# Where two value blocks of a head group stand: rows of five, or eight groups of eight rows

## The chip, the cores and the metric

The kernel runs on one core of a Trainium2 chip, in one launch. The metric is device time in microseconds. Three runs of the kernel before gave 2576.46, 2576.75 and 2577.24 us. The core has TensorE (PE), VectorE (DVE), ScalarE (ACT), GpSimd (POOL) and SyncE (SP), whose instruction queue issues nearly all transfers, and 16 DMA engines that carry them.

## The reference

Two layers, each an attention block over a cache and a gated feed-forward block, for two sequences with one new token each. Everything is float32.

```
x: (2, 1, 512)   k_cache, v_cache: (2, 8, 32768, 128)   wq: (512, 4096)   wo: (4096, 512)

x = x + A(layernorm(x));  x = x + B(layernorm(x));  and both once more, with the same weights and caches

A: q = (x @ wq) as 32 heads of 128;  each of 8 cache heads serves 4 query heads
   p = softmax(q . k * 128**-0.5);  o = p . v;  o @ wo
B: gate = x @ W_gate;  h = gate * (gate > 0) * (x @ W_up);  h @ W_down
```

There are 8 x 2 = 16 head groups (a cache head of one sequence). Each has 16.8 MB of keys and 16.8 MB of values, and both layers read them all: about 1.1 GB go from memory to the chip.

## The kernel before

`attention_reglu_decode` goes through the head groups in the order `seq`, 0 to 15 in layer 0 and 15 to 0 in layer 1, so that the last group of layer 0 is partly kept for layer 1. A head group's keys and its values come in two halves of 128 partitions x 64 KB. One half is one transfer (`pages`, line 94, with `whole`), and one transfer gives each of the 16 DMA engines eight rows. A half is worked on as four pages of 16 KB a row. Where a page is loaded by itself, it is a transfer of its own.

Order of the program: `keys(i)` (line 407) multiplies the queries into both key halves of group i; inside it stand the tail of the softmax of group i - 1 (`soft_tail`, line 248: transposes of the weights, row sums) and the output of group i - 2 (`head_out`, `project`). Then `values(i - 1, ...)` (line 434) multiplies the transposed weights `pT` of the group before into its values, with the softmax of group i behind the first page. Loads are issued by SP in program order, each when its place in the arena is free.

The arena is one tile of 220 units of 1 KB a row. `take` (line 62) gives out units: a half takes 64 of them, so 192 units are three halves in rotation; the 28 units at the end are for small tiles and for the output projection's weights. For loads, the free place that was freed longest ago is taken.

A value *block* is 512 columns (2 KB) of a value row: 128 partitions x 4 keys of 128 numbers. A half has 32 blocks, a group 64. `v_tile` (line 302) does one multiplication for each block: 16 columns of `pT` as weights, 512 columns of values, into the quarter 32c to 32c + 15 of the accumulator `acc`, where c is the block's number modulo 4.

In one group of each layer (`SIDE_HEAD` = 12, the thirteenth in order) three blocks of page 5 are not read as part of the value rows. `values` cuts the page in two pieces around them, and the second half of the group comes in five transfers: 16 KB, 8 KB, 2 KB, 16 KB and 16 KB a row. The 384 rows of these blocks come from an array of their own, `side`, laid out by the host: `load_side` (line 295) issues eight transfers of five rows of 20 KB, each to every fourth partition of a stretch of twenty, two of them ahead of each value piece from page 4 on. `side_keys` (line 265) prepares the softmax weights for those rows (GpSimd clears a part, three transposes and a masking multiplication on VectorE), and `v_side` (line 283) does ten multiplications into `acc` ahead of the last page.

Of the kernel before, what the change touches and what calls it, by code (L numbers as in the profile page):

```python
# [41 lines left out]

SIDE_HEAD, SIDE_PAGE, SIDE_AT, SIDE = 12, 5, 4, 3
SIDE_ROWS, SIDE_CHUNKS = 20, 5

C_SAME, C_SELH, C_PAIR, C_COL, C_SELQ, C_SIDE, C_END = 0, 128, 144, 176, 178, 210, 211


@with_exitstack
def attention_reglu_decode(ctx: ExitStack, tc: tile.TileContext, x, k, v, side, wq, wo, wgu, wd, consts, out):  # L50
# [28 lines left out]
    def done(loaded):  # L79
        clock[0] += 1  # L80
        for u in loaded[1]:
            freed[u] = clock[0]
# [29 lines left out]
    selq = cst[:, C_SELQ : C_SELQ + 32]  # L112
    side_rows = cst[:, C_SIDE : C_SIDE + 1]
    col = cst[:, C_COL : C_COL + NB]
# [150 lines left out]
    def side_keys(p):  # L265
        W = SIDE_CHUNKS * 32
        t = take(2 * W)
        at = SIDE_PAGE // 2 % 2 * D + (SIDE_PAGE % 2 * 8 + SIDE_AT) * 32

        def windows(rows):  # L270
            return bass.AP(rows.tensor, rows.offset + at, [rows.ap[0], [SIDE_ROWS, SIDE_CHUNKS], [1, 32]])

        def chunks(rows):
            return rows.rearrange("p (k r) -> p k r", r=32)

        nc.gpsimd.memset(t[0][64:, W:], 0.0)
        nc.vector.transpose(chunks(t[0][:, :W]), windows(p))
        for c in (0, 32):
            nc.vector.transpose(chunks(t[0][c : c + 32, W:]), windows(p[64 + c : 96 + c]))
        nc.vector.tensor_scalar_mul(t[0], t[0], side_rows[:, 0:1])  # L280
        return t

    def v_side(n, vt):
        t = side_of.pop(n)
        J = SIDE_PAGE // 4
        for k in range(2 * SIDE_CHUNKS):
            nc.tensor.matmul(
                acc[32 * (k % 4) : 32 * (k % 4) + 16, :],
                t[0][:, 32 * k + 16 * J : 32 * k + 16 * J + 16],
                vt[:, k * D : (k + 1) * D],  # L290
                start=False, stop=False,
            )
        done(t)

    def load_side(n, t):
        for c in (0, 32):
            for r in range(4):
                yield nc.sync.dma_start(t[0][c + r : c + SIDE_ROWS : 4], side[n, c // 32, r])

# [103 lines left out]
    for L in range(NLAYER):  # L403
        last = L == NLAYER - 1
        seq = list(range(NG)) if L % 2 == 0 else list(range(NG - 1, -1, -1))

        def keys(i):
            n = seq[i]
            if i < NG - 1:
                place_queries(i + 1, seq[i + 1])  # L410
            if last and i == 0:
                loads = list(kept_k)
                kept_k.clear()
            else:
                loads = pages(k, n, not (last and i == 1))
            for j, t in enumerate(loads):
                k_tile(L, i, n, j, t[0])
                if not last and i == NG - 1:
                    kept_k.append(t)
                else:  # L420
                    done(t)
                if last and i == 0:
                    yield
                if j == 1 and i >= 1:
                    soft_tail(L, seq[i - 1], i == SIDE_HEAD + 1)
# [118 lines left out]
```

## Time and profile before

| | |
|---|---|
| three runs | 2576.46 to 2577.24 us, median 2576.75 |
| span of the profiled execution | 2575.9 us |
| PE, PE weight loads | 1306.1 us (51%), 338.5 us (13%) busy |
| DVE, ACT, POOL | 149.3 us (6%), 41.1 us (2%), 3.4 us busy |
| read from memory | 1105.70 MB |

The span runs from the first to the last instruction of one profiled execution; the runs were timed apart from it, and their median is 0.85 us above it. In the profile a queue row gives packets, megabytes and the time that its packets took as a share of 16 engines' span. A DMA *packet* is one row of a transfer on one engine, or the 4-byte mark with which an engine tells that it is through with its rows. The views of a window count the packets that start in it. In the rows of instructions, `L309 PE MATMUL out<-in shapes xcount | busy, mean ns | idle before` has the engine's idle time just ahead of that group, with what ended it. `SPq` is SP's queue of issues.

### The profile page before, as it was taken

How to read it: one execution, taken by the hardware profiler on the slowest of the kernel's cores; microseconds unless marked ns; L12 is line 12 of the kernel's file. 1: busy time of each engine (PE TensorE's matmuls, PEld its weight loads, DVE VectorE, ACT ScalarE, POOL GpSimd, SP SyncE). 2: the span in 40 equal slices, each digit the busy share in tenths (PEclk: the TensorE clock that was granted, in tenths of full speed). 3: DMA queues.
4: the chain of work that ended last, by engine and by line, in shares of the span. 5: the costliest groups of instructions: out<-in, count | busy, mean ns of one | idle time of the engine just before them, and what ended most of it. 6: DMA issues, size and time to landing. Idle time of an engine off the chain costs nothing.

```text
span 2575.9 us, 19565 instructions
## 1 busy us (share of the span) xinstructions
PE 1306.1 (51%) x9256; PEld 338.5 (13%) x9256; DVE 149.3 (6%) x363; ACT 41.1 (2%) x67; POOL 3.4 (0%) x13
## 2 busy tenths in 40 slices
PE   2544454455445544545675554455445544554456
PEld 0111111111011111111121111111111101111111
DVE  0000000000000000000010000000000000000001
ACT  0000000000000000000000000000000000000000
POOL 0000000000000000000000000000000000000000
PEclk9777777777767777777778677767677777777778
DMA  9999999999999999999999999999999999999999
GB/s 425 432 430 436 430 432 436 431 432 430 434 435 429 437 431 433 420 429 426 424 416 437 430 432 436 432 434 430 434 432 431 436 431 430 436 429 422 436 424 391
DMA packets 31919, 1107.02 MB, mean 430 GB/s; under 512 B 3600, under 2 KB 3984, under 8 KB 7440
## 3 DMA queue, kind: packets, MB, share of 16 engines
q1 hardware_dynamic: 31552, 1105.61, 99.7%
q8 instruction: 72, 1.18, 0.2%
q10 hardware_dynamic: 288, 0.17, 0.0%
q14 instruction: 7, 0.06, 0.0%
HBM read 1105.70 MB, written 0.07 MB: 429 GB/s over the span
## 4 chain that ended last, share of the span: by engine, by line
DMA 68%; PE 23%; another core or an unknown queue 9%; issue 0%; DVE 0%; SPq 0%; ACTq 0%; DVEq 0%
DMA arena<-k 51%; PE sc L225 16%; DMA arena<-v 13%; PE acc L309 5%; DMA cst<-consts 2%; DMA arena<-wd 1%; DMA arena<-wq 1%; PE qp L195 1%; PE po L331 1%; DMA arena<-wgu 1%; PE op L344 0%; PE sm L257 0%; PE mp L239 0%; PE dn L384 0%
## 5 line engine op out<-in xcount | busy, mean ns | idle before, releaser
L225 PE MATMUL sc<-arena,qz 128*32 128x512 f32 x4096 | 589.7, 728 | 602.4 <-DMA arena<-k 602.4
L309 PE MATMUL acc<-arena 128*16 128x512 f32 (+1 forms) x4128 | 585.6, 720 | 587.7 <-DMA arena<-v 587.7
L225 PEld LDWEIGHTS sc<-arena,qz 128*32 128x32 f32 x4096 | 144.0, 131 | 1003.1 <-issue 689.9
L309 PEld LDWEIGHTS acc<-arena 128*16 128x16 f32 x4128 | 119.4, 109 | 1003.4 <-issue 509.9
L235 DVE TENSOR_REDUCE stat<-sc 128x1 f32<-128x1024 f32 x32 | 39.2, 1225 | 648.8 <-PE sc L225 648.8
L245 ACT ACTIVATE arena<-sc,stat 128x1024 f32<-128x1024 f32 x32 | 35.7, 1114 | 2370.3 <-DVE stat L242 2319.5
L325 DVE TENSOR_SCALAR arena<-acc,stat 128x512 f32<-128x512 f32 (+1 forms) x38 | 24.8, 665 | 779.8 <-PE acc L309 779.8
L252 DVE STREAM_TRANSPOSE arena<-arena 128x512 f32<-128x512 f32 x64 | 41.5, 687 | 2.5 <-ACT arena L245 2.5
L331 PE MATMUL po<-cst,arena 128*128 128x4 f32 x256 | 34.8, 259 | 1.9 <-DVE arena L325 1.9
L331 PEld LDWEIGHTS po<-cst,arena 128*128 128x128 f32 x256 | 32.0, 195 | 26.6 <-issue 23.5
L259 DVE RECIPROCAL stat<-sm 128x1 f32<-128x1 f32 x32 | 5.3, 166 | 435.4 <-PE sm L257 435.4
L242 DVE TENSOR_REDUCE stat<-mp 128x1 f32<-128x32 f32 x32 | 6.1, 192 | 360.5 <-PE mp L239 360.5
L362 PE MATMUL gu<-arena 128*32 128x448 f32 x128 | 20.7, 747 | 10.6 <-DMA arena<-wgu 9.4
L195 PE MATMUL qp<-arena 128*32 128x512 f32 x128 | 23.2, 838 | 4.8 <-DMA arena<-wq 2.9
L149 PE MATMUL meana<-stat,ones 128*128 128x2 f32 x4 | 0.9, 298 | 44.2 <-DVE stat L148 44.2
L239 PEld LDWEIGHTS mp<-arena,cst 128*128 128x128 f32 x64 | 13.4, 261 | 52.7 <-issue 51.0
L239 PE MATMUL mp<-arena,cst 128*128 128x32 f32 x64 | 17.3, 359 | 3.4 <-DVE arena L238 1.7
L344 PE MATMUL op<-arena,oT 128*2 128x512 f32 x112 | 14.6, 592 | 3.6 <-DVE oT L334 3.6
L257 PEld LDWEIGHTS sm<-stat,cst 128*128 128x128 f32 x64 | 9.7, 191 | 28.7 <-issue 28.7
L257 PE MATMUL sm<-stat,cst 128*128 128x1 f32 x64 | 12.4, 264 | 0.0
L334 DVE COPY oT<-po 128x4 f32<-128x4 f32 x32 | 5.2, 162 | 76.4 <-PE po L331 76.4
L384 PE MATMUL dn<-arena 128*32 128x512 f32 x32 | 6.8, 937 | 4.7 <-DVE arena L373 3.6
(62 smaller groups left out, 83.7 us busy)
## 6 DMA issues: line engine op xcount, KB each, us to landing
arena<-v SPq DMA_DIRECT2D x31, 2048.0 KB
arena<-wo SPq DMA_DIRECT2D x16, 1024.0 KB
arena<-k SPq DMA_DIRECT2D x8, 2048.0 KB
arena<-wq SPq DMA_DIRECT2D x8, 1024.0 KB
arena<-wgu SPq DMA_DIRECT2D x8, 896.0 KB
arena<-wgu SPq DMA_DIRECT2D x4, 1792.0 KB
arena<-v SPq DMA_DIRECT2D x8, 512.0 KB
arena<-wd SPq DMA_DIRECT2D x4, 1024.0 KB
```

Of the source, the lines that this page charges most:

```text
L195: nc.tensor.matmul(qp[32 * c : 32 * c + 32, B, :], xT[:, kt, :], t[0][:, c * D : (c + 1) * D], start=kt == 0, stop=kt == KT - 1)
L225: nc.tensor.matmul(sc_of[n][32 * c : 32 * c + 32, B, :], qz[:, i % 2, 28 - 4 * j : 60 - 4 * j], kt[:, ch * D : (ch + 1) * D], start=j == 0 ...
L235: nc.vector.tensor_reduce(m1[:, :1], sc_of[n], AX.XY, ALU.max)
L239: nc.tensor.matmul(mp[:, :32], same, mt[0], start=True, stop=True)
L245: nc.scalar.activation(p[0], sc_of[n].rearrange("p a b -> p (a b)"), AF.Exp, bias=nm[:, 0:1], scale=1.0, accum_out=rs[:, :1])
L252: nc.vector.transpose(pT[0][:, B * D : (B + 1) * D], p[0][:, B * D : (B + 1) * D])
L257: nc.tensor.matmul(sm[:, 0:1], same, rs[:, :1], start=True, stop=True)
L309: nc.tensor.matmul(acc[32 * c : 32 * c + 16, e * w : (e + 1) * w], pT[:, B, m, 16 * J : 16 * J + 16], vt[:, at * D + e * w : at * D + (e + ...
L325: nc.vector.tensor_scalar_mul(acs[:, t:e], acc[:, t:e], linv[:, 0:1])
L331: nc.tensor.matmul(po[:, :REP], acs[0][:, t * P : (t + 1) * P], selh[:, 4 * t : 4 * t + 4], start=t == 0, stop=t == 3)
L344: nc.tensor.matmul(op[32 * u : 32 * u + NB, :], oT[:, u, :], w, start=i == 3, stop=i == NG - 1)
L362: nc.tensor.matmul(gu[32 * j : 32 * j + 32, s, :FS], xT[:, kt, :], t[0][:, j * FS : (j + 1) * FS], start=kt == 0, stop=kt == KT - 1)
```

## The change

The one set of three blocks in one group of a layer is replaced by two blocks in each of three groups of a layer: the groups at places 3, 8 and 13 of the order in layer 0, and 4, 9 and 14 in layer 1. The blocks are now the last two of the group's last page. So the second value half stays one transfer, with rows of 60 KB instead of 64 KB, and `v_tile` does six blocks of the last page.

The rows of the two blocks stand on partitions 0 to 63 alone: each of these gets its own two blocks and those of the row 64 further on, 8 KB in all. They come as one transfer of 64 rows, issued behind the second value half; its source is an array laid out by the host as eight groups of eight rows, a little padding between the groups. `side_keys` is two transposes, which put the weights of rows 64 to 127 on partitions 0 to 63; the weights of the rows' own blocks are read from `pT`. `v_side` does four multiplications with 64 rows each, behind the group's last page. GpSimd's clearing, the masking multiplication and its constant column go.

```diff
-SIDE_HEAD, SIDE_PAGE, SIDE_AT, SIDE = 12, 5, 4, 3
-SIDE_ROWS, SIDE_CHUNKS = 20, 5
+SIDE_HEADS, SIDE = ((3, 8, 13), (4, 9, 14)), 2
+HALF_ROW = HALF * PAGE
+SIDE_ROW = HALF_ROW - SIDE * D
+SIDE_PITCH = 8 * 2 * SIDE * D + 64
...
-    def pages(src, n, whole):
+    def pages(src, n, whole, short=False):
         for h in range(NT // HALF):
             if whole:
-                t, us = load(src[n, h])
+                t, us = take(HALF_ROW, False, False)
+                w = SIDE_ROW if short and h else HALF_ROW
+                nc.sync.dma_start(t[:, :w], src[n, h, :, :w])
...
     def side_keys(p):
-        W = SIDE_CHUNKS * 32
-        t = take(2 * W)
-        at = SIDE_PAGE // 2 % 2 * D + (SIDE_PAGE % 2 * 8 + SIDE_AT) * 32
...
-        nc.gpsimd.memset(t[0][64:, W:], 0.0)
-        nc.vector.transpose(chunks(t[0][:, :W]), windows(p))
+        t = take(SIDE * 32)
+        at = 2 * D - SIDE * 32
         for c in (0, 32):
-            nc.vector.transpose(chunks(t[0][c : c + 32, W:]), windows(p[64 + c : 96 + c]))
-        nc.vector.tensor_scalar_mul(t[0], t[0], side_rows[:, 0:1])
+            nc.vector.transpose(t[0][c : c + 32], p[64 + c : 96 + c, at:])
         return t
 
     def v_side(n, vt):
         t = side_of.pop(n)
-        J = SIDE_PAGE // 4
-        for k in range(2 * SIDE_CHUNKS):
+        own = pT_of[n][0][:64, 2 * D - SIDE * 32 :]
+        for k in range(2 * SIDE):
+            keys, m = (own, k) if k < SIDE else (t[0][:64], k - SIDE)
+            c = (8 - SIDE + k) % 4
             nc.tensor.matmul(
-                acc[32 * (k % 4) : 32 * (k % 4) + 16, :],
-                t[0][:, 32 * k + 16 * J : 32 * k + 16 * J + 16],
-                vt[:, k * D : (k + 1) * D],
-                start=False, stop=False,
+                acc[32 * c : 32 * c + 16, :],
+                keys[:, 32 * m + 16 : 32 * m + 32],
+                vt[:64, k * D : (k + 1) * D],
+                start=False, stop=True,
             )
         done(t)
 
-    def load_side(n, t):
-        for c in (0, 32):
-            for r in range(4):
-                yield nc.sync.dma_start(t[0][c + r : c + SIDE_ROWS : 4], side[n, c // 32, r])
+    def load_side(L, i):
+        t = take(2 * SIDE * D, False, False)
+        e = 3 * L + SIDE_HEADS[L].index(i)
+        rows = bass.AP(side.tensor, side.offset + 8 * e * SIDE_PITCH, [[SIDE_PITCH, 8], [2 * SIDE * D, 8], [1, 2 * SIDE * D]])
+        nc.sync.dma_start(t[0][:64], rows)
+        return t
...
-                whole = pages(v, n, last or i < NG - 2)
-                if i == SIDE_HEAD:
-                    pieces[SIDE_PAGE : SIDE_PAGE + 1] = [(SIDE_PAGE, 0, SIDE_AT, None), (SIDE_PAGE, SIDE_AT + SIDE, 8, None)]
-                    whole = islice(whole, HALF)
-            sides = iter(())
+                whole = pages(v, n, last or i < NG - 2, i in SIDE_HEADS[L])
+                if i in SIDE_HEADS[L]:
+                    pieces[-1] = (NT - 1, 0, 8 - SIDE, None)
             for at, (j, lo, hi, t) in enumerate(pieces):
-                if i == SIDE_HEAD and j == HALF:
-                    aside = take(2 * SIDE_CHUNKS * D, False, False)
-                    sides = load_side(L, aside)
-                next(sides, None)
-                next(sides, None)
-                if i == SIDE_HEAD and j == NT - 1:
-                    v_side(n, aside[0])
-                    done(aside)
...
                 if soft is not None and at == 0:
                     soft_max(L, soft)
+                if i in SIDE_HEADS[L] and j == HALF:
+                    aside = load_side(L, i)
+            if i in SIDE_HEADS[L]:
+                v_side(n, aside[0])
+                done(aside)
             evacuate(L, n, i == NG - 1)
```

More of the change, by code (lines that the diff above doesn't have):

```diff
@@ L1 @@
 from contextlib import ExitStack
-from itertools import islice
 import concourse.bass as bass
@@ L112, in attention_reglu_decode @@
     selq = cst[:, C_SELQ : C_SELQ + 32]
-    side_rows = cst[:, C_SIDE : C_SIDE + 1]
     col = cst[:, C_COL : C_COL + NB]
@@ L265, in side_keys @@
     def side_keys(p):
-        W = SIDE_CHUNKS * 32
-        t = take(2 * W)
-        at = SIDE_PAGE // 2 % 2 * D + (SIDE_PAGE % 2 * 8 + SIDE_AT) * 32
[L270 to L277, printed above, removed]
+        t = take(SIDE * 32)
+        at = 2 * D - SIDE * 32
         for c in (0, 32):
-            nc.vector.transpose(chunks(t[0][c : c + 32, W:]), windows(p[64 + c : 96 + c]))
-        nc.vector.tensor_scalar_mul(t[0], t[0], side_rows[:, 0:1])
+            nc.vector.transpose(t[0][c : c + 32], p[64 + c : 96 + c, at:])
         return t
@@ L500 @@
     cst[:, C_PAIR : C_PAIR + 32] = np.equal.outer(rows // 4, np.arange(32))
-    cst[:, C_SIDE] = (rows < 64) & (rows % 32 < SIDE_ROWS)
     cst[:, C_COL : C_COL + NB] = np.equal.outer(rows % 32, np.arange(NB))
@@ L509, in by_block, with side_blocks @@
         return con(w.reshape(4, KT, 32, -1).transpose(1, 0, 2, 3)).reshape(KT, P, -1)
-    def side_blocks(vc):
-        sets = []
-        J, B, m = SIDE_PAGE // 4, SIDE_PAGE // 2 % 2, SIDE_PAGE % 2 * 8 + SIDE_AT
+    def side_blocks(v):
+        sets = np.zeros((NLAYER * 3, 8, SIDE_PITCH), np.float32)
         for L in range(NLAYER):
-            n = SIDE_HEAD if L % 2 == 0 else NG - 1 - SIDE_HEAD
-            keys = vc[n % NB, n // NB].reshape(2, 4, 2, 4, 512, DH)[J, :, B, :, 32 * m : 32 * (m + SIDE)]
-            rowsets = np.zeros((4, 4, SIDE_CHUNKS * SIDE_ROWS, DH), np.float32)
-            rowsets[:, :, : 32 * SIDE] = keys.transpose(1, 0, 2, 3)
-            t = rowsets.reshape(2, 2, 4, SIDE_CHUNKS, SIDE_ROWS // 4, 4, DH)
-            sets.append(t.transpose(1, 5, 4, 0, 3, 2, 6).reshape(2, 4, SIDE_ROWS // 4, -1))
-        return con(np.stack(sets))
+            for e, i in enumerate(SIDE_HEADS[L]):
+                n = i if L % 2 == 0 else NG - 1 - i
+                t = v[n, 1, :, SIDE_ROW:].reshape(2, 64, -1).transpose(1, 0, 2)
+                sets[3 * L + e, :, : 8 * 2 * SIDE * D] = t.reshape(8, -1)
+        return sets
     wq = con(a["A_wq"].reshape(D, 2, HKV * REP // 2, 4, 32).transpose(0, 1, 3, 2, 4)).reshape(D, -1)
@@ L528 @@
         "v": con(a["A_v_cache"].reshape(NB, HKV, 2, 4, 2, 4, 16, 32, DH).transpose(1, 0, 2, 5, 7, 4, 6, 3, 8)).reshape(NG, 2, P, SK // 2),
-        "side": side_blocks(a["A_v_cache"]),
+        "side": None,
         "wq": con(by_block(wq).reshape(KT, P, 2, -1).transpose(1, 2, 0, 3)).reshape(P, -1),
@@ L535 @@
     }
+    arrays["side"] = side_blocks(arrays["v"])
     nc = bacc.Bacc("TRN2", target_bir_lowering=False, num_devices=1, dynamic_dma_scratch_size=SCRATCH)
```

4 lines of the change are left out of this document (2 added, 2 removed).

## The prediction

> **What bounds the kernel now.** I read the page first: the DMA digits, the queues, the chain.
>
> ```profile
> span 2575.9 us, 19565 instructions
> ...
> DMA  9999999999999999999999999999999999999999
> ...
> DMA packets 31919, 1107.02 MB, mean 430 GB/s; under 512 B 3600, under 2 KB 3984, under 8 KB 7440
> ...
> q1 hardware_dynamic: 31552, 1105.61, 99.7%
> q8 instruction: 72, 1.18, 0.2%
> ...
> DMA 68%; PE 23%; another core or an unknown queue 9%; issue 0%; DVE 0%; SPq 0%; ACTq 0%; DVEq 0%
> ```
>
> The kernel's own transfers (q1) keep 16 DMA engines busy for 99.7% of the span, so what counts is how many microseconds of work the most loaded engine gets. The rate of one engine follows from the q1 row: 0.997 x 16 x 2575.9 us / 1105.61 MB = 37.17 us per MB, so 32 KB take 1.22 us, 48 KB 1.83, 64 KB 2.44, 160 KB 6.09. The q8 row is the second user: 72 transfers of 16.4 KB that carry instructions.
>
> Whether all engines are loaded alike can't be read from a mean. But the packets under 512 B are nearly all completion marks, one for each engine and transfer, so counting them in narrow windows shows how far apart the engines run. The first three windows of the DMA view are 138:139, 139:139.5 and 139.5:141 (a 128-row transfer of value rows ends there), then the q8 row of 0:138.5; the next three are 1002:1003.4, 1003.4:1006.4 and 1006.4:1009.2 (another such transfer), then the q8 row of 0:1002; then 1062.5:1066.8.
>
> ```profile
> DMA packets 27, 0.92 MB, mean 918 GB/s; under 512 B 13, under 2 KB 13, under 8 KB 13
> DMA packets 0, 0.00 MB, mean 0 GB/s; under 512 B 0, under 2 KB 0, under 8 KB 0
> DMA packets 16, 0.85 MB, mean 568 GB/s; under 512 B 3, under 2 KB 3, under 8 KB 3
> q8 instruction: 3, 0.05, 0.1%
> ...
> DMA packets 21, 0.85 MB, mean 609 GB/s; under 512 B 8, under 2 KB 8, under 8 KB 8
> DMA packets 17, 1.11 MB, mean 371 GB/s; under 512 B 0, under 2 KB 0, under 8 KB 0
> DMA packets 26, 1.18 MB, mean 421 GB/s; under 512 B 8, under 2 KB 8, under 8 KB 8
> q8 instruction: 26, 0.43, 0.2%
> ...
> DMA packets 80, 1.74 MB, mean 406 GB/s; under 512 B 18, under 2 KB 18, under 8 KB 18
> ```
>
> After three instruction transfers three engines are late. After 26 of them eight engines finish within 1002.0 to 1003.4, none for three microseconds, and the other eight at 1006.4 to 1009.2. So the instruction transfers fall on **eight engines in turn**, 26/8 = 3.25 each by then, and every core instruction that waits for a whole transfer waits for those eight. The last window says where the old five-row transfers stand: 18 marks, eight of a 128-row transfer and ten of two five-row ones, while the loaded eight are not through with the transfer ahead. So all five engines of the five-row transfers are among the eight light ones.
>
> **The price of one instruction transfer** to its engine. The window 60.5:62 has one alone:
>
> ```profile
> q8 instruction: 1, 0.02, 4.2%
> ```
>
> Its own packet takes 0.042 x 16 x 1.5 = 1.0 us. From the lateness: the middles of the two groups of marks are 1007.8 and 1002.7, 5.1 us for 3.25 transfers, 1.57 each; some of that can be an offset from the start. I take 1.5 us, near the second row, since lateness is what is paid; bounds 1.0 and 1.6. Over the run a loaded engine gets 72/8 = 9 of them: 13.5 us (9.0 to 14.4).
>
> [...]
>
> **The change, part by part.** All sums are work on one engine over both layers.
>
> ```profile
> arena<-side SPq DMA_DIRECT2D x16, 100.0 KB
> ```
>
> *Before.* In one head group of each layer three blocks of 2 KB rows leave the value rows: 8 rows x 6 KB = 48 KB less on each of 16 engines, 2 x 1.83 = 3.65 us. In their place come eight transfers of five 20 KB rows. The page's 3600 marks agree with five engines for each: 220 transfers x 16 + 16 x 5 = 3600. Those five get 160 KB a layer, 2 x 6.09 = 12.18 us. Against a kernel without any of this: loaded eight 13.5 - 3.65 = **+9.85 us**; five light ones 12.18 - 3.65 = +8.53; the other three -3.65. The loaded eight are the bound.
>
> *Removed and added transfers.* Both five-row sets and their gaps in the value rows go. In six head groups two blocks leave the last half: 8 rows x 4 KB = 32 KB less on every engine, 6 x 1.22 = 7.31 us. One transfer of 64 rows of 8 KB takes their place. Its source is written as eight groups of eight rows. By the marks, a transfer of five rows used five engines; I take eight engines with eight rows each, 64 KB, 6 x 2.44 = 14.62 us, and that they are the light ones. The other end: sixteen engines with four rows, 32 KB each.
>
> [...] The trace shows the five; no run here shows an eight yet.
>
> *The sum.* Loaded eight: 13.5 - 7.31 = +6.19. Light eight: 14.62 - 7.31 = **+7.31**. The light eight become the bound, by 1.1 us, and the end moves by 7.31 - 9.85 = **-2.54 us**. With 1.6 us an instruction transfer the old bound is 10.75 and the gain 3.44. With 1.0 the old bound is the five light engines' 8.53, and the gain 1.2; but then they, not the loaded eight, would have been last.
>
> *Number of transfers.* Eight pieces of value rows fewer (two halves that were cut in five are whole again), sixteen five-row ones fewer, six more. q1 and q8 together fill 99.9%, so the gaps are at most 0.1% x 2575.9 = 2.6 us for some 220 transfers: 0.01 us each, nothing to 0.2 us in all. I take nothing.
>
> *SP's queue.* The sixteen issues on line 298 leave, and with them a stall; then the halves:
>
> ```profile
> 1000.12 0.33 SPq L76 DMA_DIRECT2D arena<-k  x1
> ...
> 1050.72 9.93 PE L225 MATMUL sc<-arena,qz 128*32 128x512 f32 x64 [10.15 <-DMA arena<-k]
> 1050.75 19.98 SPq L298 DMA_DIRECT2D arena<-side  x2
> ...
> SPq L298 <- DMA arena<-k: 44.7, 4, 12.6
> SPq L298 <- DMA arena<-v: 43.1, 4, 18.6
> ```
>
> In the old stage SP waited 44.7 + 43.1 us on line 298 with the next value pieces queued behind it. The light engines can run dry there; the loaded ones were 3 to 7 us behind and had work, so I count nothing back. The new transfer is one issue directly behind the second value half; the next key half is queued behind it. Its 8 units come from the small end of the arena, by the allocator's oldest-freed rule either never used or last used by an output-projection tile of an earlier head pair, long read; so no wait of its own. If it did wait, the cover is the lead: the half issued at 1000.12 is first used at 1050.72, and a half of 8 x 64 KB takes 19.5 us, so 31 us of queued work cover a late issue.
>
> *TensorE.* The new multiplications run behind the last value tile of a head.
>
> ```profile
> L309 PE MATMUL acc<-arena 128*16 128x512 f32 (+1 forms) x4128 | 585.6, 720 | 587.7 <-DMA arena<-v 587.7
> L287 PE MATMUL acc<-arena 128*16 128x512 f32 x40 | 5.5, 592 | 0.0
> ...
> 328.89 47.59 DMA arena<-v
> ...
> 376.53 9.10 PE acc L309 x64
> ```
>
> Twenty calls (40 rows in the trace, two for each call) become 24, and six value blocks fewer go through line 309 (12 instead of 6 left out): two calls fewer in all. PE idles 10.15 us ahead of the half above, 587.7 us before line 309 in all; cost nothing. The side rows can land up to 2.44 us behind the last half; PE then has the 9.10 us of that half to do first. So PE does not wait for them. Uncovered, it would be at most 2.44 us in six places, 14.6 us.
>
> *VectorE and GpSimd.*
>
> ```profile
> L279 DVE STREAM_TRANSPOSE arena<-arena 32x160 f32<-32x160 f32 x4 | 1.3, 334 | 0.1
> L280 DVE TENSOR_SCALAR arena<-arena,cst 128x320 f32<-128x320 f32 x2 | 0.8, 386 | 0.2
> L277 DVE STREAM_TRANSPOSE arena<-arena 128x160 f32<-128x160 f32 x2 | 0.6, 302 | 0.0
> L276 POOL MEMSET arena<- 64x160 f32 x2 | 0.5, 227 | 163.3 <-PE acc L309 163.3
> ```
>
> 2.7 us of DVE and 0.5 of GpSimd in two places become two smaller transposes in six places, at most 12 x 0.334 = 4.0 us, 0.67 a head. They sit in front of the reciprocal and behind the two transposes that PE needs, in the 10 us before a half lands. Cost nothing; without that cover 0.67 x 6 - 2.7 = 1.3 us.
>
> *The end.* The last issue stands 2.6 us ahead of the span's end and follows the last weights; it moves with them.
>
> ```profile
> 2573.29 0.35 SPq L485 DMA_DIRECT2D out<-x  x1
> ```
>
> The sum is made against the span: 2575.9 - 2.5 = 2573.4. The runs' median is 2576.75, 0.85 above the span, and I keep that distance: **2574.2 us**. Single light engines also carry a few other instruction packets and marks, worth up to a microsecond: 2573.0 to 2575.6.
>
> **Rivals.**
> 1. *The two groups take turns*: where a layer ends everything waits for everything, and each layer has its own worst engine. A layer has up to five instruction transfers on one engine: 7.5 - 1.83 = 5.67 before; 7.5 - 3.65 = 3.85 after, and the light eight 3.65. Twice the difference: 3.65 us, 2573.1. For it: the many small weight transfers between the layers. Against it: 72/8 is nine, not ten.
> 2. *The eight engines are not the light ones* (slower). The five-row rows prove five light engines only. If the eight of the new transfer take three loaded ones, each of these has 13.5 + 7.31 = 20.8, 11.0 above the old bound: 2587.7. It decides from the first loaded engine in the set. For it: nothing names the other three. Against it: five of five were light, and sixteen engines in a light and a loaded eight are most simply the first and the last eight.
> 3. *It does not do what it says*: the 64 rows go to all 16 engines, four each. Then 32 KB come back where 32 KB left, the loaded eight stand at 13.5, 3.65 above before: 2580.4. For it: 64 divides by 16. Against it: the outer count of the source is eight.
> 4. *Instruction transfers cost the data nothing.* Then the five light engines' 8.53 was the bound, and becomes 7.31: -1.2 us, 2575.5. Against it: the eight late marks.
>
> [...]
>
> **How the numbers follow.** The forecast 0.55; rival 1 0.20; rival 2 0.07; rival 3 0.07; rival 4 0.04; 0.07 for what I don't see, half of it slower. The forecast, rivals 1 and 4 lie within 2572.4 to 2576.9 with the spread of the runs: 0.79 to 0.82, so the range is **2572.4 to 2576.9**. A measurement of this kernel can tell about 0.2% (5.2 us) from no change. Over 0.2% faster needs a gain above any of these, 0.04; over 0.2% slower is rival 2 and half of the unseen, 0.11; within 0.2% 0.85.
>
> **What would show it.** Right: six issues of 512 KB for the side rows with eight marks each (q1's marks 3600 - 80 - 8 x 16 + 6 x 8); q1 packets of 60 KB in six halves; the marks of a late transfer spread over some 3 us, with no empty gap of 3 us between two groups of eight; no SP wait on the new issue. Wrong: sixteen marks for each (rival 3); three engines that fall 2.4 us further behind the other loaded ones at each of the six places (rival 2); PE waiting for the side tile at the end of a head; a stretch where the DMA digits fall.

## The result, and the profile after

The changed kernel takes 2614.45 us (median of 4 runs, 2612.53 to 2616.64), the kernel before beside it 2576.80 us: a ratio of 1.0144, interval 1.0132 to 1.0157. It is slower by 37.7 us, where 2.5 us less had been forecast.

The page of the changed kernel, with the rows that answer to those shown of before:

```profile
span 2613.5 us, 19493 instructions
...
DMA  9999999999999999999999999999999999999998
GB/s 420 433 434 434 434 418 434 434 434 433 431 398 435 433 434 432 433 408 409 385 398 430 434 434 433 433 415 431 432 434 431 434 403 432 433 432 434 432 394 342
DMA packets 31039, 1106.95 MB, mean 424 GB/s; under 512 B 3440, under 2 KB 3824, under 8 KB 7024
...
q1 hardware_dynamic: 30672, 1105.54, 99.2%
q8 instruction: 72, 1.18, 0.2%
...
DMA 58%; PE 27%; another core or an unknown queue 14%; DVE 0%; issue 0%; SPq 0%; ACTq 0%; DVEq 0%
...
arena<-side SPq DMA_DIRECT2D x6, 512.0 KB
```

The bytes are those of before, the instruction transfers still 72, the engines still busy, and the 3440 short packets are the number worked out for eight engines in each of the six new transfers. What has changed is the rate. The row of digits doesn't show it, since an engine whose packet takes longer is as busy as ever (q1 has 98.7% in the second of the windows below, at 323 GB/s); the row of GB/s does. In the kernel before it was:

```profile
GB/s 425 432 430 436 430 432 436 431 432 430 434 435 429 437 431 433 420 429 426 424 416 437 430 432 436 432 434 430 434 432 431 436 431 430 436 429 422 436 424 391
```

Now it stands at 430 to 435 nearly everywhere and falls to 418, 398, 408, 415, 403 and 394 in six slices, those of the new transfers. It also falls further than before where layer 0 ends (409, 385 and 398 in the middle, against 426, 424 and 416) and in the last slice (342 against 391). The six issues of the changed kernel:

```profile
L292 SPq DMA_DIRECT2D arena<-side x6: 636/636/763, 329.1 to 2488.5; - x6
its engine sat idle before it (us, times) until:
who waited for it (us, times):
```

(line, operation and count; the issue's shortest, median and longest time in ns, first and last start.) SP didn't wait at the issue, and no wait for the tile is listed with it. (Among SP's own waits there is one for the landing of side rows: a load of weights on line 77 waited 3.8 us, once.) TensorE, by the rows of the new multiplications, waited for no data either, only 5.1 us of issue in all:

```profile
L280 PE MATMUL acc<-arena x48: 589/594/600, 385.9 to 2547.2; 64*16 64x512 f32 x48
its engine sat idle before it (us, times) until:
  issue: 5.1, 6
```

So the time is lost in the DMA engines, some 40 us behind each issue, when the rows are moved. Six windows of the DMA view of the changed kernel, 20 us each, from 366, 766, 1160, 1718, 2120 and 2520 us:

```profile
DMA packets 200, 7.65 MB, mean 382 GB/s; under 512 B 24, under 2 KB 24, under 8 KB 24
DMA packets 180, 6.46 MB, mean 323 GB/s; under 512 B 24, under 2 KB 24, under 8 KB 24
DMA packets 181, 6.77 MB, mean 339 GB/s; under 512 B 22, under 2 KB 22, under 8 KB 22
DMA packets 197, 7.30 MB, mean 365 GB/s; under 512 B 24, under 2 KB 24, under 8 KB 24
DMA packets 185, 6.72 MB, mean 336 GB/s; under 512 B 24, under 2 KB 24, under 8 KB 24
DMA packets 350, 6.39 MB, mean 319 GB/s; under 512 B 40, under 2 KB 40, under 8 KB 40
```

At the ordinary 433 GB/s each would hold 8.66 MB. Together 10.7 MB are missing, which is 24.6 us at that rate: two thirds of the 37.7 us are in these six stretches. (A little less: the last one holds weights in short rows as well, and the stretch from 2500 to 2520 us of the first experiment below, which does so too, has 8.30 MB.) The q1 rows agree: its packets took 99.2% of 2613.5 us, 2592.6 us an engine, against 99.7% of 2575.9, 2568.2, so 24.4 us more for the same bytes. The rest is idle time. By the records of the packets, an engine had none under way for 14.2 us on the mean, against 2.9 before; 5.5 of the 14.2 are where layer 0 ends, and 11.3 in the last slice (3.9 before). These are the places where engines that are through have nothing left while others still move rows; that is argued from the place, since the trace doesn't name an engine.

### The profile page after: what moved, and what is told of

Its sections match the earlier page's. It is cut to its first block, busy times and chain, and to the rows that moved or that the text cites. A ratio compares the mean times of both kernels' runs of the same rounds, so it can differ in the third digit from the quotient of the medians.

```text
span 2613.5 us, 19493 instructions
## 1 busy us (share of the span) xinstructions
PE 1319.8 (50%) x9240; PEld 339.1 (13%) x9240; DVE 149.4 (6%) x367; ACT 41.1 (2%) x67; POOL 3.0 (0%) x11
## 2 busy tenths in 40 slices
DMA packets 31039, 1106.95 MB, mean 424 GB/s; under 512 B 3440, under 2 KB 3824, under 8 KB 7024
## 3 DMA queue, kind: packets, MB, share of 16 engines
q1 hardware_dynamic: 30672, 1105.54, 99.2%
## 4 chain that ended last, share of the span: by engine, by line
DMA 58%; PE 27%; another core or an unknown queue 14%; DVE 0%; issue 0%; SPq 0%; ACTq 0%; DVEq 0%
DMA arena<-k 44%; PE sc L227 16%; DMA arena<-v 10%; PE acc L304 7%; DMA cst<-consts 2%; DMA arena<-wgu 1%; DMA arena<-wo 1%; PE qp L197 1%; PE po L326 1%; DMA arena<-wq 1%; PE op L339 1%; PE gu L357 0%; PE mp L241 0%; PE dn L379 0%
## 5 line engine op out<-in xcount | busy, mean ns | idle before, releaser
L304 PE MATMUL acc<-arena 128*16 128x512 f32 (+1 forms) x4104 | 595.8, 731 | 611.6 <-DMA arena<-v 611.4
L326 PEld LDWEIGHTS po<-cst,arena 128*128 128x128 f32 x256 | 32.0, 195 | 26.5 <-issue 23.5
L259 PE MATMUL sm<-stat,cst 128*128 128x1 f32 x64 | 12.4, 264 | 0.0
```

What stands on the lines that cost most here:

```text
L259: nc.tensor.matmul(sm[:, 0:1], same, rs[:, :1], start=True, stop=True)
L304: nc.tensor.matmul(acc[32 * c : 32 * c + 16, e * w : (e + 1) * w], pT[:, B, m, 16 * J : 16 * J + 16], vt[:, at * D + e * w : at * D + (e + ...
L326: nc.tensor.matmul(po[:, :REP], acs[0][:, t * P : (t + 1) * P], selh[:, 4 * t : 4 * t + 4], start=t == 0, stop=t == 3)
```

## The experiments

Each diff is against the changed kernel unless it says otherwise, and each time is a median beside runs of the kernel before on the same chip (2576.8 to 2577.6 us). A *loaded* engine is one that carries instruction transfers, a *light* one carries none. Where an expectation names theories by letters, A is that writes of two engines of the new transfer meet, B that the reads meet in the source, C that some of its eight engines are loaded. Engines are numbered as the groups of rows in a transfer's source are, since no trace names an engine. Where an expectation names runs, e1 is the first experiment, e3 the kernel without any block set aside, and e8 the first of the four kernels without padding.

**Which partitions the rows go to.** Eight engines move the 64 side rows of a place (24 marks in the window from 766 us above, 16 of them of a transfer of 128 rows), eight rows each if they share alike. By the program group e of the source goes to partitions 8e to 8e+7. The first experiment sends it to partitions 4e to 4e+3 and 32+4e to 32+4e+3, with two transfers of 32 rows at each place instead of one of 64. Here and in the expectations these are called the *own* partitions of engine e, those four further on the *next engine's*, and rows placed otherwise are on *others'*. That is a name for where the program puts a group: no trace names partitions, and that an engine has partitions of its own is not shown. What bears on it is what the kernels below cost:

```diff
-        rows = bass.AP(side.tensor, side.offset + 8 * e * SIDE_PITCH, [[SIDE_PITCH, 8], [2 * SIDE * D, 8], [1, 2 * SIDE * D]])
-        nc.sync.dma_start(t[0][:64], rows)
+        W = 2 * SIDE * D
+        for c in range(2):
+            rows = bass.AP(side.tensor, side.offset + 8 * e * SIDE_PITCH + 4 * c * W, [[SIDE_PITCH, 8], [W, 4], [1, W]])
+            nc.sync.dma_start(t[0][32 * c : 32 * c + 32], rows)
```

> [...] Theory A (destination: two engines write the same piece of on-chip memory at a time and hold everything up): the slow stretches of some 7 us at the six places go, 8 KB packets fall from up to 0.68 us to 0.31. Theory C (two of the eight engines are loaded ones): what is left is rival 2 of the prediction, 2576.8 + 11 = 2588 us, with two engines far behind. A without C: 2574. Theory B (source: the eight streams collide where they are read): unchanged, 2612 to 2617.

Measured: 2586.08 us, ratio 1.0033 (1.0020 to 1.0047), 28.4 us below the changed kernel with the same bytes from the same source addresses by as many engines (32 marks in the first window below, 16 + 2 x 8), although there is a transfer more at each place. The windows 366:386 and 766:786 of this kernel:

```profile
DMA packets 225, 8.76 MB, mean 438 GB/s; under 512 B 32, under 2 KB 32, under 8 KB 32
DMA packets 222, 8.73 MB, mean 437 GB/s; under 512 B 32, under 2 KB 32, under 8 KB 32
```

The slow stretches are gone. The source was tried by itself, with 4 KB of padding between the eight groups instead of 256 bytes:

```diff
-SIDE_PITCH = 8 * 2 * SIDE * D + 64
+SIDE_PITCH = 8 * 2 * SIDE * D + 1024
```

> The changed kernel with 4 KB instead of 256 bytes between the groups of the source array, nothing else. Theory B (the eight streams, 65792 bytes apart, collide where they are read): 2574 to 2590 us, and the slow stretches go. Theory A (destination): unchanged, 2612 to 2617.

Measured: 2615.75 us, 1.0148 (1.0128 to 1.0168), as the changed kernel. And without any block set aside:

```diff
-SIDE_HEADS, SIDE = ((3, 8, 13), (4, 9, 14)), 2
+SIDE_HEADS, SIDE = ((), ()), 2
```

> No side rows at all: every value half is a whole transfer of 64 KB rows. By the sums of the prediction the loaded eight stand at 13.5 instead of 9.85 us: 2576.8 + 3.65 = 2580.4. If instruction transfers cost the data nothing (rival 4), all engines are alike and the time is 8.5 us under before: 2568.

Measured: 2581.02 us, 1.0011 (1.0002 to 1.0021), 3.5 us above before. The prediction's sum for engines that get their rows back is 3.65.

**Are the eight engines light?** The remaining 8.6 us between the first experiment and before should be engines that carry instruction transfers. It can be seen in the first experiment's windows 1160:1164.6, 1164.6:1166 and 1166:1170, around the third place:

```profile
DMA packets 96, 1.94 MB, mean 421 GB/s; under 512 B 24, under 2 KB 24, under 8 KB 24
DMA packets 12, 0.78 MB, mean 556 GB/s; under 512 B 0, under 2 KB 0, under 8 KB 0
DMA packets 47, 1.77 MB, mean 442 GB/s; under 512 B 6, under 2 KB 6, under 8 KB 6
```

An engine of the set leaves three marks here: one for the last value rows and one for each of the two transfers. Most are through by 1164.6; then come six marks on their own, two engines with three each: in the records four packets of 8 KB stand between a mark of either engine and its next. The next kernel is the first experiment with the rows of engines 5, 6 and 7 left out, so that it computes nothing from 24 of the 64 side rows (they stay zero):

```diff
-            rows = bass.AP(side.tensor, side.offset + 8 * e * SIDE_PITCH + 4 * c * W, [[SIDE_PITCH, 8], [W, 4], [1, W]])
-            nc.sync.dma_start(t[0][32 * c : 32 * c + 32], rows)
+            rows = bass.AP(side.tensor, side.offset + 8 * e * SIDE_PITCH + 4 * c * W, [[SIDE_PITCH, 5], [W, 4], [1, W]])
+            nc.sync.dma_start(t[0][32 * c : 32 * c + 20], rows)
```

> As e1, but the side rows of engines 5 to 7 (24 of 64) are left out, so only five engines carry side rows, to their own partitions; the multiplications run over the old contents in those rows. Theory C (the loss left in e1 is that loaded engines are among 5 to 7): nobody loaded carries side rows any more, the five stand at 14.62 - 7.31 = 7.31 us, the loaded ones at 13.5 - 7.31 = 6.19, which is the sum of the prediction: 2574 us. If something else makes e1 slower than before (the number of transfers, the short rows, the multiplications with 64 rows): it stays at 2584 to 2586.

Measured: 2575.12 us, 0.9991 (0.9981 to 1.0000). Its windows at the same three times:

```profile
DMA packets 88, 1.96 MB, mean 426 GB/s; under 512 B 23, under 2 KB 23, under 8 KB 23
DMA packets 11, 0.72 MB, mean 515 GB/s; under 512 B 0, under 2 KB 0, under 8 KB 0
DMA packets 25, 1.64 MB, mean 410 GB/s; under 512 B 0, under 2 KB 0, under 8 KB 0
```

The late six are gone: both late engines are among 5, 6 and 7. The kernel before, with its transfers of five 20 KB rows made into transfers of six 16 KB rows, tries engine 5 alone:

```diff
-SIDE_ROWS, SIDE_CHUNKS = 20, 5
+SIDE_ROWS, SIDE_CHUNKS = 24, 4
```

> The kernel before with transfers of six rows of 16 KB instead of five of 20 KB, each engine to its own partitions: 128 KB a layer on six engines. If engine 5 is a light one: the loaded ones stay at 9.85 us and the time at 2576 to 2578. If it is loaded: 13.5 + 2 x (4.87 - 1.83) = 19.6, 9.7 above before, 2586.

Measured: 2585.73 us, 1.0030 (1.0018 to 1.0042), with 3616 marks, one more than before for each of the sixteen transfers: six engines. Engine 5 is loaded, and so is one of 6 and 7; which one wasn't tried.

**Other ways to share the rows out.** Five engines with eight own rows, and 24 rows over twelve engines:

```diff
+        for c in range(2):
+            rows = bass.AP(side.tensor, at + 4 * c * W, [[SIDE_PITCH, 5], [W, 4], [1, W]])
+            nc.sync.dma_start(t[0][32 * c : 32 * c + 20], rows)
+        for c in range(2):
+            rows = bass.AP(side.tensor, at + 5 * SIDE_PITCH + 12 * c * W, [[W, 12], [1, W]])
+            nc.sync.dma_start(t[0][32 * c + 20 : 32 * c + 32], rows)
```

> As e1, but 40 of the 64 side rows go through five engines (two transfers of five groups of four rows, to the engines' own partitions) and the other 24 as two transfers of twelve rows, one row for each of twelve engines. Theory C: the loaded ones among engines 5 to 7 now get 16 KB a place instead of 64; the five light engines get 80 - 32 KB, 6 x 1.78 = 10.7 us, the loaded ones at most 13.5 - 3.65 = 9.85: 0.9 us above before, 2577.6, and 10 us below e1. Without C (all eight of the new set light): e1 is at 2574 and this one 3.4 us above it.

Measured: 2593.84 us, 1.0065 (1.0048 to 1.0081). A miss: the 24 rows, which are all that it has above the run at 2575.12, cost 18.7 us. They go to partitions 20 to 31 and 52 to 63, twelve engines with one row each in either transfer (50 marks in the window 366:386, 16 + 2 x 5 + 2 x 12, at 376 GB/s). Next, all 64 rows over sixteen engines:

```diff
+        rows = bass.AP(side.tensor, side.offset + 8 * e * SIDE_PITCH, [[2 * SIDE * D, 64], [1, 2 * SIDE * D]])
```

> The 64 side rows as one transfer over all 16 engines, four rows each (the source without groups). Every engine moves as many bytes as in e3 (2581 us). [...] Without a collision: 2581.

Measured: 2607.48 us, 1.0115 (1.0095 to 1.0135), 26.5 us above the kernel without side rows and above the 2581 expected without a collision. A transfer of the same form, alone in a run below (its window 16.3:19.4), has 64 rows and sixteen marks; if each of the sixteen engines moves four rows, every engine has the same bytes in both kernels.

**A detour, and how the marks showed it.** Four kernels vary the number of rows on others' partitions, and the source, which has no padding in them. In the first, all rows are meant for the next engine's partitions:

```diff
-SIDE_PITCH = 8 * 2 * SIDE * D + 64
+SIDE_PITCH = 8 * 2 * SIDE * D
...
+        nc.sync.dma_start(t[0][4:36], bass.AP(side.tensor, at + 4 * W, [[4 * W, 8], [W, 4], [1, W]]))
+        nc.sync.dma_start(t[0][36:64], bass.AP(side.tensor, at + 36 * W, [[4 * W, 7], [W, 4], [1, W]]))
+        nc.sync.dma_start(t[0][:4], bass.AP(side.tensor, at, [[W, 4], [1, W]]))
```

> [...] Theory A as a collision of two writers: near e1, 2585 to 2591. If writing another engine's partitions is slow in itself: near the changed kernel, 2608 to 2616.

In the second the first 32 rows, in the third the first 60 are meant for own partitions:

```diff
-        nc.sync.dma_start(t[0][4:36], bass.AP(side.tensor, at + 4 * W, [[4 * W, 8], [W, 4], [1, W]]))
-        nc.sync.dma_start(t[0][:4], bass.AP(side.tensor, at, [[W, 4], [1, W]]))
+        nc.sync.dma_start(t[0][:32], bass.AP(side.tensor, at, [[4 * W, 8], [W, 4], [1, W]]))
+        nc.sync.dma_start(t[0][32:36], bass.AP(side.tensor, at + 32 * W, [[W, 4], [1, W]]))
```

> [...] If the loss is in rows that are written to the partitions of another engine's stream, and goes with their number, the time lies about halfway between those two runs (2586.1 and 2609.6): some 2598 us, 2593 to 2603. If any such transfer sets off a whole slow stretch, it is near 2609; if the loss needs more than four such rows of an engine at a place, it is near 2586. The spread of the engines' landings after the third place is then between 12 and 16 us, and the longest packets of 60 KB at a place are over 3 us for about half as long as in the run with all rows on others' partitions.

```diff
-        nc.sync.dma_start(t[0][36:64], bass.AP(side.tensor, at + 36 * W, [[4 * W, 7], [W, 4], [1, W]]))
-        nc.sync.dma_start(t[0][32:36], bass.AP(side.tensor, at + 32 * W, [[W, 4], [1, W]]))
+        nc.sync.dma_start(t[0][32:60], bass.AP(side.tensor, at + 32 * W, [[4 * W, 7], [W, 4], [1, W]]))
+        nc.sync.dma_start(t[0][60:64], bass.AP(side.tensor, at + 60 * W, [[W, 4], [1, W]]))
```

> [...] If the loss goes with the rows on others' partitions, it is 4/32 of the 20.9 us that 32 such rows cost: 2586.1 + 2.6 = 2588.7, within 2587 to 2591, and the packets at the six places are as short as in the run with all rows on their own. If any such row sets off a whole slow stretch, the time is 2600 to 2608. In between, 2592 to 2599, the length of the stretch grows with the rows, but not in proportion.

In the fourth all of them are:

```diff
+        for c in (0, 32):
+            rows = bass.AP(side.tensor, at + c * W, [[4 * W, 8], [W, 4], [1, W]])
+            nc.sync.dma_start(t[0][c : c + 32], rows)
```

> All 64 rows go to the writing engines' own partitions, as in the run at 2586.1; but the source has no padding, so that the eight engines read exactly 32 KB apart, as in the runs with 64, 32 and 4 rows on others' partitions (2609.6, 2607.0, 2606.2). If the destination causes the slow stretch, the time is 2586, 2583 to 2589, with packets of ordinary length. If the distance between the reads causes it in those three runs, the time is 2604 to 2610 here too, with packets of 60 KB above 3 us at the six places.

Measured: 2609.55 us (1.0123, 1.0103 to 1.0143), 2607.02 (1.0115, 1.0085 to 1.0144), 2606.23 (1.0113, 1.0083 to 1.0142) and 2609.84 (1.0124, 1.0094 to 1.0153). All alike, even the one that should have written own partitions only. For a while that looked like a second cause in the source. The answer is in one row of the page, here of the kernel without side rows, and below it of the last of the four:

```profile
DMA packets 30607, 1106.95 MB, mean 429 GB/s; under 512 B 3392, under 2 KB 3776, under 8 KB 6976
```

```profile
DMA packets 31183, 1106.95 MB, mean 424 GB/s; under 512 B 3584, under 2 KB 3968, under 8 KB 7168
```

3584 - 3392 = 192 marks are 32 a place, sixteen for each of two transfers, where the first experiment has eight. Rows that lie in one piece in the source are not kept in groups of four here: 32 rows went to sixteen engines, two each if they share alike, so that even the last of the four has no group of four on one engine. The other three have 3596, 34 a place: 16 + 14 + 4. So none of the four has the first experiment's groups on single engines, and they say nothing about the source or about the number of rows. Three kernels have the padding back. In the first, 60 rows go to the next engine's partitions, and the last four, still from one piece of the source, from four engines to partitions 0 to 3:

```diff
+        nc.sync.dma_start(t[0][4:36], bass.AP(side.tensor, at, [[SIDE_PITCH, 8], [W, 4], [1, W]]))
+        nc.sync.dma_start(t[0][36:64], bass.AP(side.tensor, at + 4 * W, [[SIDE_PITCH, 7], [W, 4], [1, W]]))
+        nc.sync.dma_start(t[0][:4], bass.AP(side.tensor, at + 7 * SIDE_PITCH + 4 * W, [[W, 4], [1, W]]))
```

> [...] If the destination causes the slow stretch, 2605 to 2612. [...]

The same, with those four apart too:

```diff
-SIDE_PITCH = 8 * 2 * SIDE * D + 64
+SIDE_PITCH = 9 * 2 * SIDE * D + 64
...
+        nc.sync.dma_start(t[0][:4], bass.AP(side.tensor, at + 8 * W, [[SIDE_PITCH, 4], [1, W]]))
```

> [...] If the destination alone sets off the slow stretch, 2604 to 2612. If the four rows without padding did it in the run at 2610.6, 2586 to 2591, and the destination is worth no more than the 11.8 us between the two kernels of single-row transfers.

And own partitions as in the first experiment, read at half the distance:

```diff
-SIDE_PITCH = 8 * 2 * SIDE * D + 64
+SIDE_PITCH = 4 * 2 * SIDE * D + 64
...
+            at = side.offset + (16 * e + 8 * c) * SIDE_PITCH
+            rows = bass.AP(side.tensor, at, [[SIDE_PITCH, 8], [W, 4], [1, W]])
```

> Two transfers to own partitions, as in the runs at 2586.1 (engines 64 KB + 256 B apart in the source) and 2609.8 (32 KB apart); here they are 32 KB + 256 B apart. If reads a power of two apart set off the slow stretch in the second, this one is at 2586, 2583 to 2590. If the distance has to be 64 KB or more, or the padding is not what counts, 2603 to 2612.

Measured: 2610.57 us (1.0126, 1.0097 to 1.0156), 2608.97 (1.0124, 1.0080 to 1.0167) and 2586.62 (1.0036, 1.0020 to 1.0052). Rows on the next engine's partitions cost 22.9 us more than on the own ones (2608.97 - 2586.08), at the marks that the written groups ask for (3506 = 3392 + 6 x (8 + 7 + 4) in the first two, 3488 = 3392 + 6 x 16 in the third, as in the first experiment); the distance between the reads does nothing (2586.62 against 2586.08). The window 366:386 of the second, then of the third:

```profile
DMA packets 210, 7.58 MB, mean 379 GB/s; under 512 B 35, under 2 KB 35, under 8 KB 35
```

```profile
DMA packets 224, 8.70 MB, mean 435 GB/s; under 512 B 32, under 2 KB 32, under 8 KB 32
```

**The changed kernel's exact destination, with a twin.** Two kernels have eight transfers of one row for each engine, from the changed kernel's source addresses. One writes own partitions:

```diff
+        for r in range(8):
+            rows = bass.AP(side.tensor, side.offset + 8 * e * SIDE_PITCH + r * W, [[SIDE_PITCH, 8], [1, W]])
+            nc.sync.dma_start(t[0][r % 4 + 32 * (r // 4) : 32 + 32 * (r // 4) : 4], rows)
```

> [...] If the destination counts, it is the run with two such transfers (2586.1) with 36 transfers more, at most 0.3 us each by the extra marks: 2584 to 2592. If not the destination but anything else of the changed kernel's place is slow, 2605 to 2615, like the twin below.

The other writes 8e to 8e+7:

```diff
-            nc.sync.dma_start(t[0][r % 4 + 32 * (r // 4) : 32 + 32 * (r // 4) : 4], rows)
+            nc.sync.dma_start(t[0][r:64:8], rows)
```

> The same eight transfers from the same source; engine e's rows go to partitions 8e to 8e+7, exactly where the changed kernel's engines write. If the destination sets off the slow stretch, 2608 to 2620, some 25 us above its twin with own partitions. If it is the single transfer of 64 rows (eight rows in a row on an engine, behind one set of marks), it is within 4 us of its twin.

Measured: 2597.51 us (1.0078, 1.0049 to 1.0107) and 2609.29 (1.0123, 1.0094 to 1.0153). The destination is worth 11.8 us here, half of what was expected. The first is itself 11.4 us above the run with two transfers, which was not expected either: 0.32 us for each of 36 more transfers. The window 366:386 shows idle engines there, q1 being 101.4% in the first experiment's:

```profile
q1 hardware_dynamic: 249, 7.24, 87.1%
```

Where engines already idle between single rows, part of the loss can fall into gaps; that is argued, not shown.

**The transfers alone.** Six transfers ahead of everything else in the kernel before, with nothing beside them, were to give their price: 32 rows to own partitions twice, 32 to the next engine's, 64 in groups of eight, 64 in one piece, and 32 own rows again:

```diff
+    for each in (probe_own, probe_own, probe_foreign, probe_eights, probe_sixteen, probe_own):
+        each()
```

> [...]

Measured: 2595.98 us in one run, against 2578.16 of before. The fourth of them, meant for eight engines with eight rows each, is alone in the window 11.5:14.5:

```profile
DMA packets 80, 0.52 MB, mean 175 GB/s; under 512 B 16, under 2 KB 16, under 8 KB 16
```

64 rows and sixteen marks: without padding it, too, went to sixteen engines, and of eight the run says nothing. It was repeated with padding, ahead of a kernel in which half of the rows go to own partitions:

```diff
+        nc.sync.dma_start(t[0][:32], bass.AP(side.tensor, at, [[SIDE_PITCH, 8], [W, 4], [1, W]]))
+        nc.sync.dma_start(t[0][36:64], bass.AP(side.tensor, at + 4 * W, [[SIDE_PITCH, 7], [W, 4], [1, W]]))
+        nc.sync.dma_start(t[0][32:36], bass.AP(side.tensor, at + 8 * W, [[SIDE_PITCH, 4], [1, W]]))
...
+    for each in (probe_own, probe_own, probe_next, probe_eights, probe_own):
+        each()
```

> At each place eight engines write four rows each to their own partitions (0 to 31), then seven engines four rows to the next engine's (36 to 63) and four engines one row (32 to 35). Five transfers stand alone at the start: twice 32 rows to own partitions, 32 rows to the next engine's, 64 rows as in the changed kernel, 32 own rows again; the time that the first weights are issued later for them is taken off. If the loss goes with the rows on others' partitions, the span without the transfers at the start lies halfway between the run with all rows on their own (span 2584.3) and on the next engine's (2604.9): 2594.6, within 2591 to 2598; if any such row sets off a whole stretch, 2602 to 2606. Alone, 32 own rows take four packets of 0.31 us on each engine. [...]

Measured: 2622.88 us, 1.0182 (1.0165 to 1.0199), with 3546 marks. SP's issues of the first weights are 19.66 us later than in the first experiment (20.39 against 0.73). Its windows 6.3:8.5, 10.2:12.4 and 14:19 hold, alone, 32 own rows, 32 rows on the next engine's partitions, and the changed kernel's 64 rows:

```profile
q1 hardware_dynamic: 40, 0.26, 43.4%
...
q1 hardware_dynamic: 40, 0.26, 41.2%
...
q1 hardware_dynamic: 72, 0.52, 43.9%
```

The share times 16 engines times the window's length is the time of all packets: 15.3, 14.5 and 35.1 us. In the first two 32 rows take as long on own and on the next engine's partitions. Nearly all rows but an engine's first take 309 ns in the trace of both; the first ones, about 1 us each, make up the rest. In the third the 56 later rows take (35.1 - 8 x 1.0) / 56 = 0.48 us each, and some 20 of them 0.60 to 0.65, twice 0.309. From the first row's start to the last one's end the 64 rows took 4.8 us, where eight rows of 0.309 us are 2.5; eight rows an engine on own partitions alone weren't run. So **a placement that is slow in the kernel need not be slow alone**: rows on the next engine's partitions are not (14.5 us against 15.3), and cost 22.9 us in six places beside the other transfers, while the changed kernel's 64 rows are slow with nothing beside them (0.48 us against 0.309). That the rows' writes meet fits both, but what they would meet in is not shown.

Without the 19.66 us the span is 2618.1 - 19.7 = 2598.4, 14.1 us of the 20.6 between the spans with all rows on own partitions (2584.3) and on the next engine's (2604.9), for half of the rows; it lies just above the first range and below the second. But the profiled run is the fastest of four. By the medians it is 2622.88 - 19.66 = 2603.2, 17.1 of the 22.9 us, and the span that goes with it, 1.8 less, lies 0.6 us below the second range. Either way half of the rows cost well over half of the loss, so it doesn't grow in proportion to them; whether a few rows are enough for nearly all of it, these runs leave open.

## Why the prediction was wrong, step by step

| from | to | us | cause |
|---|---|---|---|
| before 2577.3 | 40 of the 64 side rows, none by engines 5 to 7, own partitions 2575.1 | -2.1 | no loaded engine in the set: the predicted bound, in a kernel that leaves rows out |
| before 2577.5 | all 64 rows, own partitions 2586.1 | +8.6 | two loaded engines in the set |
| 2586.1 | changed kernel 2614.5 | +28.4 | group e on partitions 8e to 8e+7, not on its own |

(The changed kernel was timed beside 2576.8 us, the first experiment beside 2577.5.)

- *The failed step* is "Removed and added transfers": "I take eight engines with eight rows each, 64 KB, 6 x 2.44 = 14.62 us, and that they are the light ones." The eight engines were right, by the 3440 marks. The price was taken from the kernel's mean rate, 37.17 us per MB on an engine; with the rows on partitions 8e to 8e+7 the six places cost 28.4 us more than on the own ones, 4.7 each, and engines that move no side rows were slow there too. Nothing in the working asks which partitions the rows go to. The diff shows the difference: line 298 of the kernel before wrote every fourth partition, so that row e fell on 4e + r or 32 + 4e + r; the new transfer writes them in order. The other end that the prediction gives for this term, too, is a matter of how many engines there are, not of where the rows go: for sixteen engines rival 3 has 2580.4 us, and the run with sixteen took 2607.5.
- *"that they are the light ones"* failed as well, on two of the eight engines. Rival 2 had the mechanism, with 0.07, and worked out 11.0 us for as little as one loaded engine; 8.6 were measured with two, and why it is 2.4 less no run here shows. The argument against it, that two groups of eight are most simply the first and the last eight, was a guess about an order that no row showed.
- *The removed rows* hold: with nothing set aside the time is 3.5 us above before, where 3.65 were worked out, which also takes rival 4 away; rival 3, sixteen engines, is not what the marks show. That run doesn't weigh an instruction transfer by itself. An estimate can be made from the run at 2575.1: if its five light engines, at 7.31 us, are the bound, the old bound was 7.31 + 2.14 = 9.45 us, and one transfer costs (9.45 + 3.65) / 9 = 1.46, near the 1.5 that was taken. Engine 5 as a sixth engine of the old transfers got 8 x 16 KB in each layer, 9.75 us in all by the prediction's rate, where a loaded engine had none; 8.5 were measured (2585.73 - 2577.26).
- *The sum itself*, freed of the two errors, came out as far as can be told: 2.1 us below before (interval of the ratio 0.9981 to 1.0000), where 2.5 were worked out.
- *Number of transfers*: the working took at most 0.01 us each from the engines' mean share. Between eight engines with single rows, 0.32 us each were measured. It decided nothing here, but the bound was no bound.
- *SP, TensorE, VectorE* behaved as said: no wait on the new issue, none for the side tile.
- *"a stretch where the DMA digits fall"* was too blunt a sign: the digits stayed at 9 while the rate in 20 us fell by up to a quarter.

Three things stay open: why packets of engines that move no side rows are slow at these places too (the records show it: a packet of 64 KB takes 2.42 us elsewhere, but in the windows from 766 and 2120 us 15 or 16 such packets of over 3 us are under way at once, and only eight engines move side rows); what makes one placement slower than another, and how the 28.4 us divide into what the rows of the transfer cost each other and what they cost beside other transfers; and which of engines 6 and 7 is loaded. No kernel run here computes everything and beats the kernel before.

## What to carry to other kernels

Before pricing a transfer to part of the partitions by the kernel's mean rate, try it with more than one placement of its rows, and beside the transfers it will run with; sending group e to partitions 4e to 4e+3 and 32+4e to 32+4e+3 instead of 8e to 8e+7 was worth 28.4 us here at equal bytes. Count the completion marks of every variant: they tell how many engines a transfer used, which its written shape does not (32 rows written as eight groups of four left eight marks from a padded source, sixteen from one without padding). A DMA engine that is busy all the time need not work at full rate (98.7% busy at 323 GB/s in one window, where 433 is ordinary); read GB/s in narrow windows.

## What the hardware showed that was not expected

- 512 KB written as group e to partitions 8e to 8e+7 slowed the whole core to 319 to 382 GB/s for 20 us at a place, engines without side rows among them (up to 16 packets of 64 KB at once above 3 us, 2.42 elsewhere); on the own partitions the six places have 415 to 446 GB/s. The changed kernel's rows have packets of up to 0.65 us even when they stand alone, against 0.31 for 32 rows on own partitions.
- The distance between the reads made no difference: 256 bytes or 4 KB behind 64 KB gave 2614.5 and 2615.8 us, and 32 KB or 64 KB between the engines (with 256 bytes) 2586.6 and 2586.1.
- Instruction transfers load engine 5 (adding 256 KB to it cost 8.5 us) and one of 6 and 7, but none of 0 to 4 (2575.1 us with side rows on these alone): with the numbers of the groups of rows, the eight engines that carry them are no block of eight.
